# Rows scattered in expert order with token number and gate inside, in a sigmoid-attention, mixture-of-experts and feed-forward chain on one Trainium2 core

## The chip, the core and the metric

One core of a Trainium2 chip runs the whole program. TensorE (PE) multiplies, ScalarE (ACT) and VectorE (DVE) work on the tiles, GpSimd (POOL) does small work and starts the indirect transfers, SyncE (SP) starts the others. Each engine takes its instructions strictly in the order in which they stand; a wait holds up all that stands behind it on that engine. The metric is the device time of one execution in microseconds (us), the median of several runs.

## The reference, cut to what matters

```python
# 4 batches, 12 heads, 448 tokens, head size 64; 1792 tokens of 768 numbers; 8 experts, 1024 wide; FFN 2048 wide
attn = 1 / (1 + exp(-(q @ k.T / 8 - log(448))))
x = rows(attn @ v)                                  # 1792 x 768
logits = normalize(x) @ normalize(expert_emb).T / tau
e = argmax(logits);  gate = softmax(logits)[e]
for each expert e: out[mask] = gate[mask] * (relu(x[mask] @ w1[e]) @ w2[e])
h = out @ w_in;  return (h - tanh(h)) @ w_out
```

All products are done in two-part float32 (a high and a low part, three matmuls for one product).

## The kernel before, in words

**Attention.** 24 pairs of heads, six for each batch, cut into 84 units. A unit is six score matmuls (L230), two sigmoids on ACT (`ah` L237 and `pq` L238), one subtraction on DVE (`al`, L239) and six matmuls with v (L253) three units later. The `al` instructions are a good ruler: one for each unit, counted here from 1 to 84. After each pair its output is turned into token rows (`rows`, L270): PE writes `pr`, DVE copies it into `rec` (112 partitions x 4 rows x 768).

**Routing.** When a batch's sixth pair is done, `route_a` (L394) finds each token's expert; `square` sums squares on ACT; `route_b` (L416) ranks the tokens within their expert with small matmuls (`prank`) and gives `idx`; `gate` (L444) works out the gate. Before, SP writes `rec` to the DRAM table `x_tok` in token order, one further transfer of single words writes the gate behind each row (L466), and POOL scatters the token number, single words again, to `id_reg` in expert order (L441). `ROUTE` and `ROUTE_E` say how many units after `route_a` this is placed; `ROUTE_E` is for the third batch.

**Experts.** Tokens are worked on in groups of 256 of one expert. Two groups are taken from the first three batches, before the fourth is routed (`plan_early`, `early_rows`); the plan for the others (`plan`, L561) is made during the first group. `gather_rows` (L642) fetches, for each half group of 128: the token numbers `gi` from `id_reg`, then the rows `xg` from `x_tok` by these numbers, both indirect from POOL; then ACT multiplies the row by its gate (L658), and SP writes the numbers to `tok_d`, 128 single words. `columns` (L663) transposes the rows on PE, ACT writes the high part `xh` and DVE the low part `xl`. A group (L730) is then 14 products: eight with w1 (18 matmuls each) and six with w2 (24 each), 288 matmuls; for each, ACT casts the weights (`wh`), DVE makes the rest (`wl`), and four such pairs of buffers go round, so ACT is at most four products ahead of PE. In this input nine groups run. SP loads the weights: seven transfers for each group (`w1raw`, `w2raw`).

**What sets the order.** The engines' programs come from a scheduler that simulates the program; only PE's order in the attention is written by hand (units, `plan(u, f)`). While the groups run, ACT and DVE also convert the weights of the last stage (`conv_steps`, L801: `cr` loaded by SP, `ca` on ACT, four steps on DVE, written back). The last stage (`ffn`, L844) reads `toki`, the token numbers in the order of the rows, and scatters the output by it.

Of the kernel before, what the change touches and what calls it, by code (L numbers as in the profile page):

```python
# [10 lines left out]
F32 = mybir.dt.float32  # L11
# [12 lines left out]
ROUTE, ROUTE_E = 8, 8  # L24
# [14 lines left out]
class Prog:  # L39
    def __init__(self, ctx, tc, q, k, v, emb, tau, w1, w2, w_in, w_out, out):  # L40
# [9 lines left out]
        self.R = self.DM + 1  # L50
# [8 lines left out]
    def constants(self):  # L59
# [20 lines left out]
        self.e_off = cp.tile([P, E], F32, name="e_off")  # L80
        nc.gpsimd.iota(self.e_off, [[self.NT, E]], base=0, channel_multiplier=0, allow_small_or_imprecise_dtypes=True)
        self.base = cp.tile([P, E], F32, name="base")
        nc.vector.tensor_copy(self.base, self.e_off)
        self.tok = cp.tile([CP, self.B, NCH], I32, name="tok")
        nc.gpsimd.iota(self.tok, [[self.S, self.B], [1, NCH]], base=0, channel_multiplier=NCH)
# [41 lines left out]
    def attention(self):  # L127
# [93 lines left out]
        def scores(u):  # L221
# [16 lines left out]
            nc.scalar.activation(pv, pv, AF.Sigmoid, **sc)  # L238
            nc.vector.tensor_tensor(lo, pv, f32(hi), ALU.subtract)  # L239

        def av(u):
            hi, lo = tiles.pop(u)
            for x, (i, a, c, o) in enumerate(slots[u]):
# [12 lines left out]
                if e:  # L256
                    b, j = pairs[i]
                    if j == 0:
                        self.bts[b] = dict(
                            rec=xp.tile([CP, NCH, NJ * P], F32, tag="rec", name="rec"),  # L260
                            ss=self.sm.tile([CP, NCH], F32, tag="ss", name="ss"),
                            u=xp.tile([CP, NCH, E], F32, tag="u", name="u"),
                        )
# [6 lines left out]
        def rows(i):  # L270
# [19 lines left out]
            if j >= NJ - 2:  # L290
                c0, c1 = (0, (NJ - 1) * P) if j < NJ - 1 else ((NJ - 1) * P, NJ * P)
                self.x_dma = nc.sync.dma_start(self.x_rows(b)[:, :, c0:c1], rec[:, :, c0:c1])

        def square(bt, c):
            sq = xp.tile([CP, NJ * P], F32, tag="sq", name="sq", bufs=1)
            nc.scalar.activation(sq, bt["rec"][:, c], AF.Square, accum_out=bt["ss"][:, c : c + 1])
# [19 lines left out]
        for i in range(NK):  # L316
            kqs.append(pers.tile([P, KW + S], F32, name=f"kq{i}"))
        kpads()
# [13 lines left out]
        with tc.manual_schedule(engines=pe):  # L332
# [11 lines left out]
            def route(i):  # L344
# [6 lines left out]
                if b == B - 2:  # L351
                    plan(now[0] + ROUTE_E, self.route_b, b, r, pr)
                    plan(now[0] + ROUTE_E, self.gate, b, r)
                    plan(now[0] + ROUTE_E, self.early_rows)
                    plan(ns + 1, self.early_columns, lambda: ps2.tile([P, 2, 512], F32, tag="qk", name="xt"))
                elif b < B - 1:
                    plan(now[0] + ROUTE, self.route_b, b, r, pr)
                    plan(now[0] + ROUTE, self.gate, b, r)
# [57 lines left out]
    def route_b(self, b, st, pst):  # L416
# [6 lines left out]
        for c in range(NCH):  # L423
# [3 lines left out]
            )  # L427
        rk = sm.tile(A3, F32, tag="rk", name="rk")
        nc.vector.tensor_tensor(rk, pr[:CP, :NCH], self.base[:CP].unsqueeze(1).to_broadcast(A3), ALU.add)
        nc.vector.tensor_tensor(rk, rk, oh, ALU.mult)  # L430
        idx = sm.tile([CP, NCH], I32, tag="idx", name="idx")
        with nc.allow_low_precision(reason="whole numbers below 2**24"):
            nc.vector.tensor_reduce(idx, rk, AX.X, ALU.add)
        nc.vector.tensor_tensor(self.base, self.base, pr[:, NCH], ALU.add)
        for c in range(NCH):
            self.scatter(
                self.id_sc,
                out=self.id_reg,
                out_offset=bass.IndirectOffsetOnAxis(ap=idx[:, c : c + 1], axis=0),
                in_=self.tok[:, b, c : c + 1],  # L440
# [3 lines left out]
    def gate(self, b, st):  # L444
# [19 lines left out]
        gt = sm.tile([CP, NCH], F32, tag="gt", name="gt")  # L464
        nc.vector.reciprocal(gt, gs)
        nc.sync.dma_start(self.x_rows(b)[:, :, DM : DM + 1], gt.unsqueeze(2))  # L466

    def x_rows(self, b):
        return self.x_tok[b * self.S : (b + 1) * self.S].rearrange("(p c) r -> p c r", c=NCH)
# [611 lines left out]
```

## Time and profile before

| | before |
|---|---|
| runs shown | 1087.98, 1092.14, 1100.88 us (median 1092.14) |
| profiled execution | 1099.0 us, its span 1097.3 us |
| PE busy in the span | 1028.9 us (94%) |
| mean granted TensorE clock | 0.975 of full speed |
| attention | to about 242 us |
| first expert product starts | 255.36 us |
| last stage starts | 614.55 us |

In the rows below a timeline line is: start, duration, engine, source line, operation, output <- inputs, shape, count, and in brackets the idle time ahead of it with what ended it. All times are us from the start of the span.

### The profile page before, as it was taken

How to read it: one execution, taken by the hardware profiler on the slowest of the kernel's cores; microseconds unless marked ns; L12 is line 12 of the kernel's file. 1: busy time of each engine (PE TensorE's matmuls, PEld its weight loads, DVE VectorE, ACT ScalarE, POOL GpSimd, SP SyncE). 2: the span in 40 equal slices, each digit the busy share in tenths (PEclk: the TensorE clock that was granted, in tenths of full speed). 3: DMA queues.
4: the chain of work that ended last, by engine and by line, in shares of the span. 5: the costliest groups of instructions: out<-in, count | busy, mean ns of one | idle time of the engine just before them, and what ended most of it. 6: DMA issues, size and time to landing. Idle time of an engine off the chain costs nothing. (4 is left out here: it accounts for less than half of the span.)

```text
span 1097.3 us, 16753 instructions
## 1 busy us (share of the span) xinstructions
PE 1028.9 (94%) x6418; PEld 952.1 (87%) x6418; DVE 816.6 (74%) x1093; ACT 557.7 (51%) x693; POOL 185.5 (17%) x191
## 2 busy tenths in 40 slices
PE   6999999867899979979999899999999999999996
PEld 4777777657899979979999799999999999999996
DVE  7888888926578677768886479988898766667773
ACT  6788878636457556556665353344343333322320
POOL 7446454522141111200000000000000300000002
PEclk9999999987989989989999899999999999999999
DMA  5443534069988999999692455444442533322312
GB/s 164 136 133 52 161 51 147 7 58 270 245 224 190 295 260 244 200 200 234 225 317 88 147 201 173 173 173 157 176 134 110 194 137 116 113 93 111 116 58 101
DMA packets 93400, 175.11 MB, mean 160 GB/s; under 512 B 14976, under 2 KB 72064, under 8 KB 93312
## 3 DMA queue, kind: packets, MB, share of 16 engines
q1 hardware_dynamic: 89664, 161.35, 50.4%
q0 software_dynamic: 3648, 12.61, 5.3%
q8 instruction: 53, 0.87, 0.3%
q14 instruction: 35, 0.29, 0.1%
HBM read 156.55 MB, written 36.26 MB: 176 GB/s over the span
## 5 line engine op out<-in xcount | busy, mean ns | idle before, releaser
L953 PE MATMUL o<-wo,gh 128*128 128x384 f32 x896 | 240.5, 335 | 0.7 <-DVE acc L963 0.7
L913 PE MATMUL z<-yh,wi 128*128 128x448 f32 x768 | 222.0, 371 | 4.5 <-ACT yh L888 4.5
L953 PEld LDWEIGHTS o<-wo,gh 128*128 128x128 f32 x896 | 162.9, 188 | 2.3 <-DVE acc L963 1.0
L913 PEld LDWEIGHTS z<-yh,wi 128*128 128x128 f32 x768 | 145.2, 190 | 17.2 <-ACT yh L888 4.7
L953 PE MATMUL o<-wo,gl 128*128 128x384 f32 x448 | 149.8, 334 | 0.0
L725 PE MATMUL pth<-xh,wh 128*128 128x256 f32 x432 | 126.4, 293 | 17.4 <-DVE hl L742 13.4
L913 PE MATMUL z<-yl,wi 128*128 128x448 f32 x384 | 138.3, 368 | 0.0
L725 PE MATMUL pth<-xh,wl 128*128 128x256 f32 x432 | 125.3, 290 | 1.4 <-DVE wl L716 1.4
L725 PE MATMUL pth<-xl,wh 128*128 128x256 f32 x432 | 125.3, 290 | 0.0
L725 PE MATMUL pty<-hh,wh 128*128 128x256 f32 x432 | 122.3, 288 | 2.8 <-ACT hh L741 2.8
L725 PE MATMUL pty<-hl,wh 128*128 128x256 f32 x432 | 122.7, 286 | 1.9 <-DVE hl L742 1.9
L725 PE MATMUL pty<-hh,wl 128*128 128x256 f32 x432 | 122.7, 286 | 0.6 <-DVE wl L716 0.6
L963 DVE TENSOR_TENSOR acc<-o,acc 128x768 f32<-128x768 f32 x98 | 93.6, 955 | 39.5 <-PE o L953 38.3
L239 DVE TENSOR_TENSOR al<-pq,ah 128x896 fp32r<-128x896 f32 x84 | 90.4, 1084 | 34.7 <-ACT pq L238 34.5
L473 POOL DMA_INDIRECT out_dram<-acc,toki x14 | 17.3, 1232 | 577.2 <-DVE acc L963 577.2
L936 ACT CAST gh<-r 128x896 fp32r<-128x896 f32 x32 | 30.1, 941 | 156.6 <-DVE r L934 80.6
L237 ACT ACTIVATE ah<-pq,bias_s 128x896 fp32r<-128x896 f32 x84 | 85.4, 1016 | 41.2 <-PE pq L230 39.8
L725 PEld LDWEIGHTS pth<-xh,wh 128*128 128x128 f32 x432 | 86.1, 199 | 18.8 <-issue 14.2
L716 DVE TENSOR_TENSOR wl<-w1raw,wh 128x768 fp32r<-128x768 f32 x72 | 68.6, 956 | 31.6 <-ACT wh L715 31.1
L716 DVE TENSOR_TENSOR wl<-w2raw,wh 128x1024 fp32r<-128x1024 f32 x54 | 66.1, 1223 | 31.0 <-ACT wh L715 30.6
L725 PEld LDWEIGHTS pth<-xh,wl 128*128 128x128 f32 x432 | 85.8, 199 | 1.9 <-DVE wl L716 1.9
L715 ACT CAST wh<-w2raw 128x1024 fp32r<-128x1024 f32 x54 | 56.5, 1048 | 58.9 <-PE pty L725 24.4
(210 smaller groups left out, 2196.7 us busy)
## 6 DMA issues: line engine op xcount, KB each, us to landing
w1raw<-in_moe_w_dram SPq DMA_DIRECT2D x36, 768.0 KB
w2raw<-in_moe_w_dram SPq DMA_DIRECT2D x27, 1024.0 KB
wi<-dwi SPq DMA_DIRECT2D x32, 768.0 KB
wo<-dwo SPq DMA_DIRECT2D x32, 768.0 KB
cr<-in_moe_w_in_dram SPq DMA_DIRECT2D x16, 768.0 KB
dwi<-cr SPq DMA_DIRECT2D x16, 768.0 KB
cr<-in_moe_w_out_dram SPq DMA_DIRECT2D x16, 768.0 KB
dwo<-cr SPq DMA_DIRECT2D x16, 768.0 KB
```

Of the source, the lines that this page charges most:

```text
L237: nc.scalar.activation(hi, pv, AF.Sigmoid, **sc)
L239: nc.vector.tensor_tensor(lo, pv, f32(hi), ALU.subtract)
L473: i = self.nc.gpsimd.indirect_dma_start(**kw)
L715: nc.scalar.copy(wh, cols)
L716: nc.vector.tensor_tensor(wl, cols, f32(wh), ALU.subtract)
L725: nc.tensor.matmul(pt[:, u], a[:, kk], b[:, kk], start=(n == 0), stop=(n == 3 * K - 1))
L913: nc.tensor.matmul(z[:, g, :GT], wi[:, a, j * P : (j + 1) * P], b[:, j], start=(n == 0), stop=(n == 3 * NJ - 1),)
L936: nc.scalar.copy(gv, r)
L953: nc.tensor.matmul(o[:, w, :NW], a[:, u, i * P : (i + 1) * P], wo[:, b, w * NW : (w + 1) * NW], start=(n == 0), stop=(n == 3 * CH - 1),)
L963: nc.vector.tensor_tensor(acc[i], ov, acc[i], ALU.add)
```

## The change

Rows are no longer written to `x_tok` in token order. `rec` gets 16 more words in each row: word 768 is the token's number, word 769 its gate. POOL scatters these rows of 3136 bytes straight to their place in the batch's expert order (`send_rows`), so SP's writes of `rec`, of the gates and the table `id_reg` go away, and a gather needs one hop, not two. The place of a token in the new table has to be worked out from four batches' tables (`row_of`). The number comes back by a transpose of one column (`row`), and SP writes it as one line of 256 words. `gather_rows` is split: for the first two groups the fetching (`gather_x`) and the multiplication by the gate (`gate_rows`) are placed apart. The weights of the first group no longer wait for its rows. `ROUTE_E` goes from 8 to 3.

```diff
-ROUTE, ROUTE_E = 8, 8
+ROUTE, ROUTE_E = 8, 3
-        self.R = self.DM + 1
+        self.R = self.DM + 16
 # attention: rows()
-            if j >= NJ - 2:
-                self.x_dma = nc.sync.dma_start(self.x_rows(b)[:, :, c0:c1], rec[:, :, c0:c1])
+            if j == 0:
+                nc.gpsimd.tensor_copy(rec[:, :, self.DM : self.DM + 1], self.tok[:, b].unsqueeze(2))
 # route()
-                    plan(now[0] + ROUTE_E, self.gate, b, r)
+                    plan(now[0] + ROUTE_E - 1, self.gate, b, r)
+                    plan(now[0] + ROUTE_E, self.send_rows, b, r)
                     plan(now[0] + ROUTE_E, self.early_rows)
+                    plan(ns, self.early_gates)
+    def send_rows(self, b, st):
+        for c in range(NCH):
+            self.scatter(self.x_sc, out=self.x_tok[: (b + 1) * self.S],
+                out_offset=bass.IndirectOffsetOnAxis(ap=bt["idx"][:, c : c + 1], axis=0), in_=bt["rec"][:, c], ...)
 # gate()
-        nc.sync.dma_start(self.x_rows(b)[:, :, DM : DM + 1], gt.unsqueeze(2))
+        nc.vector.reciprocal(bt["rec"][:, :, DM + 1 : DM + 2], gs.unsqueeze(2))
+    def row_of(self, res, pos, shifts, befores, tmp):
+        V.tensor_copy(s, shifts[0])
+        for x, n in zip(shifts[1:], befores):
+            V.tensor_tensor(d, x, s, ALU.subtract)
+            V.tensor_tensor(y, pos, n, ALU.is_ge)
+            V.tensor_tensor(d, d, y, ALU.mult)
+            V.tensor_tensor(s, s, d, ALU.add)
+        V.tensor_tensor(res, pos, s, ALU.add)
 # plan(): 12 tables are picked from, not 5
+        tabs += [self.shift[:, b] for b in range(B)] + [self.n_before[:, b] for b in range(1, B)]
 # early_rows()
-            self.weight(self.e0, None, c, self.s0["g"])
+            self.weight(self.e0, None, c)
+        for s in (self.s0, self.s1):
+            for h in range(2):
+                self.gather_x(s, h, nt)
+    def early_gates(self):
+        with self.tc.issue_after(self.last_sig.ins):
+            for h in range(2):
+                self.gate_rows(self.s0, h)
 # gather_rows()
-            nc.gpsimd.indirect_dma_start(out=gi[:, h : h + 1], out_offset=None, in_=self.id_reg, ...)
-            nc.sync.dma_start(self.tok_d[o].unsqueeze(1), gi[:, h : h + 1])
 # columns()
+            nc.tensor.transpose(pt[:, h * P : (h + 1) * P], s["x"][:, h, self.DM : self.DM + 1], self.ident)
+        nc.vector.tensor_copy(s["row"], pt)
+    def keep_numbers(self, s):
+        nc.sync.dma_start(self.tok_d[o].unsqueeze(0), s["row"])
 # experts(): for the second group, after the third relu of the first
+        def second():
+            with tc.issue_after(relus[-2].ins):
+                for h in range(2):
+                    self.gate_rows(self.s1, h)
+            self.columns(self.s1, pst)
```

On SP, after the attention's last load of v (`vr`), there stands before:

```order
L183 DMA vr<-in_v_dram 128x512
L466 DMA x_tok<-gt 448x1x1
...
L660 DMA tok_d<-gi 128x1 x2
L660 REGISTER_ALU
L660 DMA tok_d<-gi 128x1
L660 ISA
L660 DMA tok_d<-gi 128x1
L686 ISA
L686 DMA w1raw_144<-in_moe_w_dram 128x6x256
```

and now, where `pe_eo` is the first group's expert from `plan_early`:

```order
L186 DMA vr<-in_v_dram 128x512
L663 TENSOR_LOAD pe_eo_2231
L663 ISA x2
L753 ISA
L753 DMA w1raw_146<-in_moe_w_dram 128x6x256
L753 ISA
L753 DMA w1raw_147<-in_moe_w_dram 128x6x256
L753 ISA
L753 DMA w1raw_148<-in_moe_w_dram 128x6x256
```

The first weights stand directly behind the plan; the four writes of single words ahead of them are gone. On ACT, at the end of the attention, the multiplications by the gate (`xg<-xg`) stand before between the sigmoids of the last two units, and the second group's two ahead of the first group's `xh`:

```order
L658 ACTIVATE xg<-xg 128x768
L237 ACTIVATE ah<-pq,bias_s 128x896
L238 ACTIVATE pq<-pq,bias_s 128x2x448
L658 ACTIVATE xg<-xg 128x768
L237 ACTIVATE ah<-pq,bias_s 128x896
L238 ACTIVATE pq<-pq,bias_s 128x2x448
L658 ACTIVATE xg<-xg 128x768 x2
L676 CAST xh<-xt 128x512 x3
L266 COPY xT<-pav 128x448
L715 CAST wh<-w1raw_144 128x768 x2
```

and now:

```order
L240 ACTIVATE ah<-pq,bias_s 128x896
L241 ACTIVATE pq<-pq,bias_s 128x2x448
L240 ACTIVATE ah<-pq,bias_s 128x896
L241 ACTIVATE pq<-pq,bias_s 128x2x448
L706 ACTIVATE xg<-xg 128x768 x2
L729 CAST xh<-xt 128x512 x3
L269 COPY xT<-pav 128x448
L776 CAST wh<-w1raw_146 128x768 x2
```

No sigmoid stands behind a gathered row, and the second group's multiplications have moved into the first group. On ACT, from the second group's end to the third group's start (`yT` takes a group's result, `xh` is the third group's input), there stands before:

```order
L715 CAST wh<-w1raw_144 128x768
L658 ACTIVATE xg<-xg 128x768 x2
L715 CAST wh<-w1raw_144 128x768
L758 ISA
L758 COPY yT_2686<-pty 128x2x256
L676 CAST xh<-xt 128x512 x2
L715 CAST wh<-w1raw_145 128x768
L813 ACTIVATE ca<-cr 128x768
L715 CAST wh<-w1raw_145 128x768
L758 ISA
L758 COPY yT_2687<-pty 128x2x256
L676 CAST xh<-xt 128x512
```

and now:

```order
L776 CAST wh<-w1raw_147 128x768
L706 ACTIVATE xg<-xg 128x768 x2
L776 CAST wh<-w1raw_147 128x768
L821 ISA
L821 COPY yT_last<-pty 128x2x256
L729 CAST xh<-xt 128x512 x2
L883 ACTIVATE ca<-cr 128x768
L706 ACTIVATE xg<-xg 128x768
L729 CAST xh<-xt 128x512
```

The first two `xh` have moved behind the second group's last `yT`, and a conversion step and one gated row stand ahead of the third.

## Rows read from the trace of the kernel before

**Rows 1.** Page, part 1: busy time, share of the span, instructions.

```profile
PE 1028.9 (94%) x6418; PEld 952.1 (87%) x6418; DVE 816.6 (74%) x1093; ACT 557.7 (51%) x693; POOL 185.5 (17%) x191
```

**Rows 2.** Timeline of PE, end of the attention and first expert group.

```profile
233.04 0.66 PE L253 MATMUL pav<-ah,vh 128*128 128x448 f32 x1 [3.42 <-ACT ah L237]
...
250.63 2.15 PE L278 MATMUL pr<-ien,xT 128*112 128x136 f32 x8 [8.72 <-ACT xT L266]
255.36 0.58 PE L725 MATMUL pth<-xh,wh 128*128 128x256 f32 x1 [2.57 <-ACT wh L715]
```

**Rows 3.** Timeline of ACT, same stretch.

```profile
231.16 0.93 ACT L658 ACTIVATE xg<-xg 128x768 f32<-128x768 f32 x1 [7.58 <-DMA xg<-x_tok,gi]
...
246.62 0.94 ACT L658 ACTIVATE xg<-xg 128x768 f32<-128x768 f32 x1 [9.10 <-DMA xg<-x_tok,gi]
...
254.48 1.57 ACT L715 CAST wh<-w1raw 128x768 fp32r<-128x768 f32 x2 [3.90 <-DMA w1raw<-in_moe_w_dram]
```

**Rows 4.** Timeline of SP's queue, same stretch.

```profile
219.59 24.15 SPq L660 DMA_DIRECT2D tok_d<-gi  x4
243.97 2.20 SPq L686 DMA_DIRECT2D w1raw<-in_moe_w_dram  x3
```

**Rows 5.** Stretches: us, busy us (instructions) of PE, PEld, DVE, ACT, POOL; clock, DMA share, GB/s.

```profile
250.00:260.00 10.00, 6.59 (x27) 5.96 (x28) 5.72 (x11) 5.21 (x9) 0.00 (x0) 0.50 0.88 248
...
500.00:540.00 40.00, 40.00 (x337) 40.00 (x336) 32.12 (x39) 24.96 (x35) 0.00 (x0) 1.00 0.80 218
```

**Rows 6.** Timeline of DVE, third batch's routing: `al` 70 and 71, gate, plan, `al` 78, plan.

```profile
189.09 2.08 DVE L239 TENSOR_TENSOR al<-pq,ah 128x896 fp32r<-128x896 f32 x2
...
203.86 0.17 DVE L465 RECIPROCAL gt<-gs 112x4 f32<-112x4 f32 x1
...
208.99 3.06 DVE L541 TENSOR_SCALAR pe_start<-pe_oh,pe_m 128x8 f32<-128x8 f32 x1
...
213.26 1.08 DVE L239 TENSOR_TENSOR al<-pq,ah 128x896 fp32r<-128x896 f32 x1
214.26 0.14 DVE L519 TENSOR_REDUCE pe_mx<-pe_left 128x1 f32<-128x8 f32 x1
...
215.64 0.22 DVE L555 TENSOR_TENSOR pe_ord<-c_tri,pe_oh 128x64 f32<-128x64 f32 x1
```

**Rows 7.** Timeline of POOL, third batch's scatter and first gather.

```profile
206.11 0.96 POOL L473 DMA_INDIRECT id_reg<-tok,idx  x1 [0.30 <-issue]
...
209.58 2.37 POOL L199 TENSOR_TENSOR w1l<-kq,w1h 128x448 fp32r<-128x448 f32 x2
...
219.83 0.94 POOL L654 DMA_INDIRECT xg<-x_tok,gi  x1 [0.74 <-DMA gi<-id_reg,gidx]
```

**Rows 8.** Transfers into `xg`: us from issue to landing.

```profile
DMA to landing us min/median/max: 7.2/10.4/19.4
```

**Rows 9.** Transfers out to `out_dram`, 128 rows of 3072 bytes: from issue to landing.

```profile
DMA to landing us min/median/max: 3.0/3.4/4.4
```

**Rows 10.** Timeline of PE in the expert groups: a set of transposes, two idle times.

```profile
298.89 0.39 PE L725 MATMUL pth<-xh,wh 128*128 128x256 f32 x1 [1.40 <-ACT wh L715]
...
383.79 1.03 PE L672 MATMUL xt<-ident,xg 128*128 128x128 f32 x8
...
475.78 0.55 PE L725 MATMUL pth<-xh,wh 128*128 128x256 f32 x1 [7.42 <-DVE hl L742]
```

**Rows 11.** Timeline of ACT in the expert groups: two waits for transfers.

```profile
401.08 0.89 ACT L813 ACTIVATE ca<-cr 128x768 f32<-128x768 f32 x1 [5.87 <-DMA cr<-in_moe_w_out_dram]
...
472.39 0.94 ACT L658 ACTIVATE xg<-xg 128x768 f32<-128x768 f32 x1 [8.42 <-DMA xg<-x_tok,gi]
```

**Rows 12.** Timeline of POOL in the expert groups: two gathers' issues.

```profile
305.63 4.87 POOL L654 DMA_INDIRECT xg<-x_tok,gi  x1 [11.24 <-DMA x_tok<-gt]
...
452.97 1.52 POOL L654 DMA_INDIRECT xg<-x_tok,gi  x1 [0.30 <-issue]
```

**Rows 13.** Waits of SP's queue over the span: total us, times, longest.

```profile
SPq L660 <- DMA tok_d<-gi: 60.4, 11, 8.3
```

More of the change, by code (lines that the diff above doesn't have):

```diff
@@ L567, in plan @@
         tn = t("tn", P, 2, E)
[L568 to L569 removed]
+        V.tensor_tensor(tn[:, 1], self.n_before[:, self.B], self.start, ALU.subtract)
         gt = t("gt", P, E, MT)
@@ L605, in plan @@
         gidx = cp.tile([P, NG, 2], I32, name="gidx")
-        V.scalar_tensor_tensor(gidx, b2(ef), float(NT), pos, ALU.mult, ALU.add)
+        self.row_of(
+            gidx, pos, [b2(sums[:, 5 + b]) for b in range(B)], [b2(sums[:, 5 + B + b]) for b in range(B - 1)],
+            t("ro", P, 3, NG, 2),
+        )
         e_i, new, off = (cp.tile([P, NG], I32, name="pl_" + x) for x in ("ei", "new", "off"))
@@ L678, in columns, with weight @@
         s["xt"] = (xh, xl)
-    def weight(self, e, new, c, after=None):
+        pt = pst()[:1, 0, :GR]
+        for h in range(2):
+            nc.tensor.transpose(pt[:, h * P : (h + 1) * P], s["x"][:, h, self.DM : self.DM + 1], self.ident)
+        s["row"] = self.mrow.tile([1, GR], F32, tag="row", name="row")
+        nc.vector.tensor_copy(s["row"], pt)
+    def keep_numbers(self, s):
+        nc, pl = self.nc, s["pl"]
+        o = slice(0, self.GR)
+        if "off" in pl:
+            o = ds(self.reg(nc.sync, pl["off"], s["slot"], self.NT - 1), self.GR)
+        nc.sync.dma_start(self.tok_d[o].unsqueeze(0), s["row"])
+    def weight(self, e, new, c):
         nc = self.nc
@@ L689, in weight @@
         self.last_w = i
-        if after is not None:
-            self.tc.add_manual_dep(
-                i.ins, after.ins.name,
-                mybir.DependencyInfo(mybir.DependencyClass.Sync, mybir.DependencyReason.DATA),
-                reason="rows of the first group before its weights",
-            )
     def experts(self, cx):
@@ L734, in group @@
                 if c >= have:
-                    with tc.issue_after(self.x_dma.ins) if mid is not None else ExitStack():
-                        self.weight(e, new, c)
+                    self.weight(e, new, c)
                 pt = ps.tile([P, 2, GR], F32, tag="h", name="pth")
@@ L780, in last_route @@
             self.route_b(*self.last_route, pst)
+            self.gate(*self.last_route)
+            self.send_rows(*self.last_route)
             pl.update(self.plan())
-            self.gate(*self.last_route)
-        group(self.s0, self.e0, None, slice(0, GR), NWE, lambda: self.columns(self.s1, pst), True, last_route)
+        def second():
+            with tc.issue_after(relus[-2].ins):
+                for h in range(2):
+                    self.gate_rows(self.s1, h)
+            self.columns(self.s1, pst)
+        group(self.s0, self.e0, None, slice(0, GR), NWE, second, True, last_route)
         e, new = (self.reg(nc.sync, self.pl1[x], 0, n) for x, n in (("e", E - 1), ("new", 1)))
@@ L1010, in build @@
                 self.attention()
-            yp = self.pool("yT", 1, side="right")
-            self.yT = [yp.tile([P, 2, self.NT + self.GR], F32, name=f"yT{c}") for c in range(self.NJ // 2)]
+            yp = self.pool("yTb", 1, side="right")
+            self.yT = [yp.tile(ysh, F32, name=f"yT{c}") for c in range(self.NJ // 2 - 1)] + self.yT
             with ExitStack() as cy:
```

142 lines of the change are left out of this document (83 added, 59 removed).

## The prediction, as it went on record

> **What bounds the kernel now.** The page's first part comes first: PE is busy 94% of the span [rows 1], so all that this change can win, short of removing PE work, lies in PE's idle time and in its slow clock. The timeline of PE from the attention's end to the first expert product [rows 2] shows where that is. PE starts a unit late by 3.42 us because ACT had not yet made `ah`; it waits 8.72 us for `xT`, again ACT's; and the first expert product, at 255.36, comes 2.57 us late for ACT's `wh`. So ACT's timeline is read next [rows 3]. ACT itself had nothing to do: at 231.16 it stood 7.58 us, and at 246.62 another 9.10 us, at a multiplication whose row was still in flight, and the sigmoids, the copy of `xT` and the casts stand behind that wait on its queue. Then it waits 3.90 us for the first weights. SP's timeline says why these are late [rows 4]: four writes of token numbers hold the queue from 219.59 for 24.15 us (each waits for its `gi`), and `w1raw` goes out only at 243.97. While PE stood, the clock granted to it fell: 0.50 of full speed in the stretch 250 to 260, against 1.00 in the middle of the groups [rows 5]. There PE does 337 matmuls in 40.00 us, so the 288 of a group take 34.2 us, and nine groups 308. From the first expert product to the last stage (255.36 to 614.55 in the table above) are 359 us: some 51 us are transposes, idle time and half clock. Of them the largest stall is 7.42 us at 475.78 [rows 10], when ACT had stood 8.42 us for a row [rows 11] whose gather POOL issued at 452.97 [rows 12] and which landed 19.4 us later [rows 8].
>
> **The change, step by step.** The sum is made for the profiled execution, 1099.0 us, which lies 6.9 above the median of the runs.
>
> (a) *The way to the first expert product.* ACT's two waits inside the attention go, since no sigmoid stands behind a gathered row any more, and SP's wait ahead of `w1raw` goes with the four writes: the weights are in place some 20 us earlier. What is left is the rows' own way, now: all of the third batch's routing, plan included, gate, four scatters, two gathers, two multiplications, transposes. It begins later than before. Before, the gate was ready at 203.86 and POOL scattered the numbers at 206.11 [rows 6, 7]; now the gate must be inside the row, and in DVE's order its reciprocal stands behind `al` 78, with 85 small operations of routing and plan between `al` 70 and `al` 78 where 33 stood. Before, `al` 78 ran at 213.26; from `al` 70 at 189.09 that is 24.2 us for eight units [rows 6]. The 52 more small operations cost 0.106 us each by the fourteen from 214.26 to 215.64, 5.5 us in all, if nothing hides them; nothing, if DVE had that much slack and no port stall like the 3.06 us of `pe_start` at 208.99, which ran beside POOL's `w1l` [rows 6, 7]. I take four of the 5.5 (DVE is close to full there): gate at 217.3, bounds 213.3 and 222. Four scatters of 0.96 + 0.30 us [rows 7] end at 222; the last lands after 3.4 us, as transfers of 128 rows to `out_dram` do [rows 9], up to 10.4, as gathers do [rows 8]; I take 4, hence 226, since a scatter of rows is most like the former. The two gathers of the first group go out 1.26 apart and need 7.2 to 10.4 [rows 8]; I take 9: the second is there at 236.3. Before, from the last gated row at 246.62 to the first product it is 8.74 us, of which ACT waited 3.90 and PE 2.57 for the weights [rows 2, 3]: without them 4.84 by ACT, 6.17 by PE at half clock. I take 5.5. But there the first group's transposes stood ready; now twelve of them follow the row, at 1.03 / 8 = 0.13 us, 1.5 us [rows 10]. 236.3 + 5.5 + 1.5 gives a first product at 243.3, **-12 us**. With the gate at 222 and landings of 10.4 for scatter and gathers it is 222 + 5 + 10.4 + 1.3 + 10.4 + 7 = 256: +1. With 213.3 and landings of 3.4 and 7.2 it would be 237, where PE's own work is the bound: its last units, two times `pr` and the transposes reach to some 240: -15.
>
> (b) *Numbers by transposes.* Two more in each of nine groups, at full cost on PE: 18 x 0.13 = **+2.3** [rows 10].
>
> (c) *Gathers of the later groups.* One hop instead of two. The row of group five that landed after 19.4 us is asked for without first fetching its number, so about 3.7 us earlier (an issue of 1.52 and the wait for the number, which in a quiet queue is 2 to 4). Of the 7.42 us and some 2 us at half clock behind it, I take half back: **-5**; bounds 0 (the landing is slow again) and -9.4.
>
> (d) *Waits for transfers in the groups.* SP spent 60.4 us of its queue's time in waits for `gi` [rows 13]; with nine line writes of a row that DVE has already made this goes nearly to nothing, and the weights and `cr` behind them leave when their buffers are free. Waits that such transfers end: 5.87 us of ACT at 401.08 for `cr` [rows 11], behind the 1.40 of PE at 298.89 [rows 10] and several like it. I take **-6**; bounds 0, since the buffers and not SP may set the time of issue (DMA engines are busy 0.80 of the middle of the groups [rows 5]), and -12.
>
> (e) *The third group's start.* Its `xh` now stand behind the second group's last `yT`, with a conversion step and a gated row ahead of the third; the plan's `gidx` come later. Nothing covers that: PE has no product of another group there. Two casts, a gate of 0.94 and `ca` of 0.89 [rows 11] are 3 to 5 us on the path: **+5**; bounds 0 and +12 (a gather that lands in 10.4 instead of 7.2, and a half clock after the stall).
>
> (f) *Longer plan on DVE.* Some 25 operations for `row_of`, about 0.2 us each with what lies between (0.22 at 215.64 [rows 6]), behind DVE's work at 32.12 of 40.00 us [rows 5]: hidden but for **+1**; 5 without cover.
>
> Sum: -12 + 2.3 - 5 - 6 + 5 + 1 = -14.7, so 1084 for an execution like the profiled one. Part of the stalls in (c) and (d) is late landings, which differ between executions; I take 4 us of them as absent in the median one. That leaves -10.7 from 1092.1: **1081 us**.
>
> A page speaks against the four scatters from POOL. The Trainium skill, page "SBUF — State Buffer", section "SBUF: two separate sides", says that the descriptors of a transfer issued by GpSimd are written by GpSimd itself, through a port pair that VectorE can hold for a whole instruction, so that such a transfer may sit waiting for VectorE. The issue of 0.96 us at 206.11, in a stretch in which DVE is nearly full, does not show it; that of 4.87 us at 305.63 [rows 7, 12] might. By the page the issues would be longer where DVE is busy; the rival C below has the time.
>
> **The rivals.** *B, the rows come no earlier.* The scatter waits for a gate that stood 13 us earlier before, and each row makes two trips of 3 KB where a number made one. With the gate at 222 and a landing of 10.4 for the gathers alone, the first product starts at 222 + 5 + 4 + 1.3 + 10.4 + 7 = 250: -6 instead of -12, and with half of (c) and (d) the sum is about -6 + 2.3 - 5 + 5 + 1 = -3: 1089. This is also the case in which the change doesn't do what it says. For it: DVE's eight units took 24.2 us already. Against: the first weights' 3.90 us go in any case.
>
> *C, slower: POOL's issues stretch.* Six indirect issues stand one behind the other ahead of the first group. At 4.87 us each [rows 12] in place of 1.26 they take 22 us more: first product at 265, +10, sum +7 with all else as forecast, and +18 with nothing of (c) and (d): 1099 to 1110. It decides from about 12 / 6 = 2 us more for each issue, where the gain of (a) is gone. For it: one issue of 4.87 and one of 1.52. Against: 0.94 and 0.96 at 204 to 220, in the same stretch [rows 7].
>
> *D, ACT is held at the head of each later group.* The gates of groups three to six stand in ACT's program some products ahead of the group's end, and all of ACT's casts stand behind them. A landing of 19.4 [rows 8] instead of 10.4 costs 3 to 7 us a group; over four groups +12 to +28 less the 7.42 already paid: 1085 to 1101. It decides when landings near 19 us are the rule rather than the longest.
>
> **How the numbers follow.** The forecast (first product 240 to 247, later stalls reduced) has 0.5, B 0.25, C 0.1, D 0.15. The likeliest gives 1081, its own range is 1070 to 1087: from (a) at -15 with (c) and (d) near their better ends, to (a) at -9 with a little less of (c) and (d). The range reaches up through B and the lower half of D: 1066 to 1096, leaving out C, the upper half of D, and a little below. About 1% is what a measurement of this kernel can tell from no change: 1081.2 and 1103.1 are the borders. Since the forecast lies at the first of them, faster takes some six tenths of its 0.5 and a part of B and D where the group's waits shrink more: 0.45. Slower is most of C and a third of D: 0.14; the rest 0.41.
>
> **What would show it.** (a) PE's idle time behind `ah` and `xT` is gone and the first expert product starts near 243; POOL's scatters begin near 217 and take about 1 us each; `w1raw` is issued near 220. If the first product starts after 250, B or C holds: B if the gate is late or the landings are long, C if the issues are. (c) No idle of 7 us ahead of a later group's `xh`. (d) SP waits little at the number writes; ACT's waits for `cr` under 2 us. (e) The third group's first product comes up to 5 us late. The forecast is wrong as a whole if DVE between `al` 70 and `al` 78 takes over 35 us, if a scatter of rows lands after 15, or if the groups, from first product to the last stage, take more than the 359 us of before.

## The result, and the profile after

The changed kernel takes 1057.4 us (median of 1055.1 to 1058.5) against 1096.3 for the kernel before beside it (1088.0 to 1100.9): a ratio of 0.965, 95% interval 0.958 to 0.972. The forecast was 1081 with a range of 1066 to 1096. The direction was right and the size was not: 39 us were gained where 11 were forecast. The kernel before was timed again beside each of the six sets of experiments below, at 1105.1 to 1117.7; the changed kernel in its second timing took 1057.2 us. Why the kernel before varies so much between sets, and the changed one does not, no run tells. Each experiment is compared with the kernel before of its own set, by the ratio, and with the 1057 of the changed kernel, which mostly comes from another set.

Busy time of the engines in the span, after (the answer to [rows 1]):

```profile
PE 1019.5 (96%) x6437; PEld 943.1 (89%) x6437; DVE 828.6 (78%) x1170; ACT 558.7 (53%) x693; POOL 175.3 (17%) x178
```

The timeline of PE, the first expert product and the longest idle time in the groups (answers to [rows 2, 10]):

```profile
238.76 1.18 PE L281 MATMUL pr<-ien,xT 128*112 128x136 f32 x8 [0.68 <-ACT xT L269]
239.69 0.37 PE L786 MATMUL pth<-xh,wh 128*128 128x256 f32 x1
...
314.79 0.50 PE L786 MATMUL pth<-xh,wh 128*128 128x256 f32 x2 [1.17 <-ACT xh L729]
```

The first product comes at 239.69, 15.7 us earlier, and the last stage starts at 575.30. In the nine groups PE waits 1.17 us at most, once, at the third group's start; ahead of the last stage it waits 5.13 us (4.54 before). The way to the first product, on POOL (last scatter, first group's two gathers), ACT (their gates) and SP (first weights), answers to [rows 3, 4, 7]:

```profile
223.02 0.94 POOL L491 DMA_INDIRECT x_tok<-rec,idx  x1 [0.30 <-issue]
227.60 0.99 POOL L698 DMA_INDIRECT xg<-x_tok,gidx  x1 [2.19 <-DMA x_tok<-rec,idx]
228.90 0.96 POOL L698 DMA_INDIRECT xg<-x_tok,gidx  x1 [0.30 <-issue]
```

```profile
231.75 0.94 ACT L706 ACTIVATE xg<-xg 128x768 f32<-128x768 f32 x1
233.15 0.94 ACT L706 ACTIVATE xg<-xg 128x768 f32<-128x768 f32 x1 [0.46 <-issue]
```

```profile
198.14 1.59 SPq L753 DMA_DIRECT2D w1raw<-in_moe_w_dram  x3
```

ACT waits for no row and no weight. SP's queue, however, stands as long at the number writes as before (60.4 us, [rows 13]), now for the row of numbers:

```profile
SPq L745 <- DVE row L737: 67.2, 8, 32.0
```

The time went like this, in the profiled executions; the third column is an experiment, told of below, in which only the distance of the numbers in DRAM differs from the kernel before:

| | before | after | before, words 64 bytes apart |
|---|---|---|---|
| first expert product | 255.4 | 239.7 | 238.1 |
| nine groups, to the last stage | 359.2 | 335.6 | 334.8 |
| last stage | 482.7 | 481.5 | 483.0 |
| span | 1097.3 | 1056.8 | 1055.8 |

### The profile page after: what moved, and what is told of

It is laid out like the page before. It is cut to its first block, busy times and chain, and to the rows that moved or that the text cites. A ratio compares the mean times of both kernels' runs of the same rounds, so it can differ in the third digit from the quotient of the medians.

```text
span 1056.8 us, 16798 instructions
## 1 busy us (share of the span) xinstructions
PE 1019.5 (96%) x6437; PEld 943.1 (89%) x6437; DVE 828.6 (78%) x1170; ACT 558.7 (53%) x693; POOL 175.3 (17%) x178
## 4 chain that ended last, share of the span: by engine, by line
issue 56%; PE 31%; DVE 7%; POOL 2%; DMA 2%; ACT 1%; POOLq 0%; SPq 0%; DVEq 0%; ACTq 0%
PE pth L786 9%; PE pty L786 9%; PE pav L256 7%; PE pq L233 5%; POOL out_dram L491 2%; DVE al L242 1%; PE pr L281 1%; DMA xg<-x_tok,gidx 1%; DVE vh L210 1%; PE xt L725 1%; DMA cr<-in_moe_w_in_dram 1%; ACT wh L776 0%; DVE xT L271 0%; ACT sq L298 0%; POOL vl L211 0%
## 5 line engine op out<-in xcount | busy, mean ns | idle before, releaser
L786 PE MATMUL pth<-xh,wh 128*128 128x256 f32 x432 | 122.6, 285 | 2.7 <-ACT xh L729 1.2
L786 PE MATMUL pth<-xh,wl 128*128 128x256 f32 x432 | 122.3, 283 | 0.3 <-DVE wl L777 0.3
L786 PE MATMUL pth<-xl,wh 128*128 128x256 f32 x432 | 122.2, 283 | 0.0
L995 ACT ACTIVATE t<-z 128x896 f32<-128x896 f32 x32 | 29.4, 920 | 112.3 <-PE z L988 75.8
L786 PEld LDWEIGHTS pth<-xh,wh 128*128 128x128 f32 x432 | 82.7, 192 | 3.3 <-ACT xh L729 1.4
```

Of the source, the lines that this page charges most:

```text
L786: nc.tensor.matmul(pt[:, u], a[:, kk], b[:, kk], start=(n == 0), stop=(n == 3 * K - 1))
```

## Experiments

**First set: which part gave the groups 23.6 us?** Four kernels, the kernel before at 1117.7 us. The theories A to M in the expectations have letters of their own; they are not the rivals B to D of the prediction. Of each edit the lines that matter are shown.

The numbers written again as single words from the gathered rows:

```diff
+        self.nc.sync.dma_start(self.tok_d[o].unsqueeze(1), s["x"][:, h, self.DM : self.DM + 1])
-            self.keep_numbers(s)
```

> The changed kernel, but the token numbers go to tok_d as before: 128 single words from each half group, written by SP straight from the gathered rows, so that SP waits for each gather (the transposes of the numbers stay, their row isn't written). Three theories of where the groups' 23.6 us came from (335.6 us from the first expert product to the last stage, 359.2 before). A, SP's waits for gathered rows hold the weights and cr behind them: +10 to +18 us, the groups at 346 to 354 us, with PE idle again behind ACT's waits for cr. B, single words are expensive for the DMA engines that carry them: +8 to +15, but as much in the run with words that wait for nothing. C, the second hop of a gather made rows late and held ACT: within 2 us of the changed kernel, 1055 to 1060.

Measured: 1104.5 us, ratio 0.988 (0.985 to 0.991). Of the 60 us by which this set's kernel before is slower than the changed kernel 47 are back, 2.6 times the most that a theory had allowed. First product 239.4, groups 385.4. SP hardly waits for rows (1.4 us); it waits 44.0 us for the landing of its own words.

Words that wait for nothing, added to the changed kernel:

```diff
+                self.nc.sync.dma_start(self.junk[k : k + P].unsqueeze(1), self.ident[:, :1])
```

> The changed kernel with work added: for each half group SP also writes 128 single words, from a constant tile to a place of its own, so that nothing is waited for. Every other engine's program is as in the changed kernel. A (SP's waits): within 2 us, 1055 to 1060. B (single words load the DMA engines): +8 to +15, the groups at 344 to 351 us, and the DMA share in the groups several hundredths up. C (second hop): within 2 us.

Measured: 1070.7 us, but not as meant: since the source is ready early, SP issued all 18 transfers at 23.6 to 64.7, among the attention's first loads. The groups stayed at 335.8, and the attention lost the time: first product 252.3. So it says nothing of words in the groups, but 2304 words that nobody reads or waits for cost 12.6 us there.

The second hop back:

```diff
+        self.nc.gpsimd.indirect_dma_start(out=gi, out_offset=None, in_=self.id_reg,
+            in_offset=bass.IndirectOffsetOnAxis(ap=s["pl"]["gidx"][:, s["slot"], h : h + 1], axis=0))
-            in_offset=bass.IndirectOffsetOnAxis(ap=s["pl"]["gidx"][:, s["slot"], h : h + 1], axis=0),
+            in_offset=bass.IndirectOffsetOnAxis(ap=gi, axis=0),
```

> The changed kernel with the second hop back: each half group's indices are first fetched, indirectly, as 128 single words from a table that holds 0, 1, 2 and so on, and the rows are then fetched by what came back. Output unchanged. First expert product 4 to 8 us later for the hop (all theories). In the groups: A (SP's waits): nothing, total 1061 to 1066. B (single words): about +4, half of the words of before come back. C (second hop makes rows late and holds ACT): +9 to +15, PE idle 2 to 8 us ahead of xh of some groups, total 1070 to 1080.

Measured: 1065.5 us, some 8 over the changed kernel. First product 240.2, groups 340.8, with one idle time of 5.21 us ahead of a group's transposes. Theory C falls: the hop costs the groups 5 us, and is not where 23.6 us went.

The kernel before without its writes to `tok_d`:

```diff
-            nc.sync.dma_start(self.tok_d[o].unsqueeze(1), gi[:, h : h + 1])
```

> The kernel before without its 18 writes of single words to tok_d: the table is filled once at the start with 0, 1, 2 and so on (so the last stage's output rows go to wrong places; the work is the same). SP no longer waits for gi. A (SP's waits): the first product 2 to 5 us earlier, groups 12 to 18 us shorter, total 1073 to 1083. B (single words): groups 4 to 8 us shorter, total 1083 to 1090. C (second hop): groups the same but for the buffer of gi, which no longer waits for the write, total 1085 to 1095.

Measured: 1068.6 us, ratio 0.957 (0.952 to 0.961). The kernel without the writes sends its output to wrong rows, with the same work otherwise. Eighteen transfers of half a kilobyte each are worth 49 us to the kernel before. First product 245.6, groups 337.1. What remained to be found was what in them costs so much.

**Second set: the wait or the words?** By now I had read [rows 13] again. Its 60.4 us are not waits for `gi`: the row names `tok_d<-gi`, the landing of the write before, at places of the same table. The wait for `gi` has a row of its own, here from the same view:

```profile
SPq L660 <- DMA gi<-id_reg,gidx: 3.7, 2, 2.9
```

In SP's timeline a second half's number write follows the first's after 13 us; other transfers go out between, and for the last 2.9 us the queue waits for the first write to land:

```profile
316.02 0.37 SPq L660 DMA_DIRECT2D tok_d<-gi  x1
...
329.04 0.35 SPq L660 DMA_DIRECT2D tok_d<-gi  x1
```

> The changed kernel itself, beside the three that follow, since the kernel before was 1117.7 us beside the first four experiments and 1096.3 before that. All theories: 1055 to 1062 us. If the kernel before depends on the chip through its waits for single words and the changed one does not, this stays at 1057 while the kernel before moves.

Measured: 1057.2 us, ratio 0.956 (0.953 to 0.960), the kernel before at 1106.0.

One write for each group in the kernel before:

```diff
-            nc.sync.dma_start(self.tok_d[o].unsqueeze(1), gi[:, h : h + 1])
+        nc.sync.dma_start(self.tok_d[o].rearrange("(h p) -> p h", p=P), gi)
```

> The kernel before with one write of numbers for each group instead of two: the same 256 single words, the same gathers ahead of it, but no second write that has to wait until the first one has landed. D (SP is held by a write that waits for the landing of the write before it, at places of the same table): SP's waits for tok_d fall from 60 us to under 15, and the time comes near that of the kernel without these writes, 1065 to 1085. B (the words themselves load the DMA engines): at most 8 us below the kernel before. A as I first put it (SP waits for gi): at most 5 us below the kernel before, since gi is waited for as ever.

Measured: 1079.7 us, ratio 0.978 (0.974 to 0.982); SP's waits for `tok_d` fell to 11.5 us. About half of the gain, with as many words: between D and B. But it does not separate the two: the two words of one partition now stand side by side in the transfer and 128 words apart in DRAM, so their order is another too.

Words from the gathered rows, each to a place of its own:

```diff
+        self.nc.sync.dma_start(self.junk[k : k + P].unsqueeze(1), s["x"][:, h, self.DM : self.DM + 1])
```

> The changed kernel with work added: SP writes the number of each gathered row as single words, as in the run with words in tok_d, so that it waits for every gather, but each to a place of its own, so that no write waits for another. D (wait of write on write): 1057 to 1066, SP waits for xg and little else. A (waits for gathered rows): near the run with words in tok_d, +30 to +47, 1090 to 1105. B (words): +5 to +15.

Measured: 1081.8 us, ratio 0.978 (0.974 to 0.982). No write waits for a write, SP's waits for rows are 6.8 us in all, and still it is 25 us slower.

Words behind the line of numbers:

```diff
+            nc.sync.dma_start(self.junk[k : k + P].unsqueeze(1), f32(s["xt"][0][:, h, :1]))
```

> The changed kernel with work added: 256 single words for each group, written behind the line of numbers from a tile that is ready then, each to a place of its own, so that SP waits for nothing more (the earlier run of this kind issued its words during the first attention units and not in the groups). D: 1057 to 1062. A: 1057 to 1062. B (words load the DMA engines): +5 to +15, DMA share in the groups up.

Measured: 1060.0 us, +3. As many words cost 3 or 25 us, by where they stand. Left were the wait for rows, and the loads among which the words go out.

**Third set: that wait alone, words among loads alone, and two parts of the way to the first product.** The kernel before at 1105.1 us.

```diff
+        self.nc.sync.dma_start(self.junk[k : k + 16].unsqueeze(0), s["x"][:1, h, self.DM : self.DM + 16])
```

> The changed kernel with a small transfer added at the places of the run whose words were written from the gathered rows to places of their own: for each half group SP writes 16 words of one row, 64 bytes, to a place of its own, so SP waits for each gather as in that run, but no 128 words follow. E (a wait of SP for gathered rows is what cost that run its 25 us): 1075 to 1085. F (the words cost it, by what they do to the loads between which they stand): 1056 to 1062.

Measured: 1056.4 us. SP waits 45.9 us for gathered rows, and it costs nothing:

```profile
SPq L704 <- DMA xg<-x_tok,gidx: 45.9, 8, 25.4
```

E falls, and with it theory A, that waits for rows hold up the loads behind them.

```diff
+                if c < 2:
+                    nc.sync.dma_start(self.junk[k : k + P].unsqueeze(1), f32(hh[:, 2 * c, :1]))
```

> The changed kernel with 256 single words added for each group, as in the earlier run with words behind the line of numbers (+3 us), but written from the first two activations of the group (hh), so that they stand among the loads of weights and cr, and not behind them; SP waits for no gather. E: 1056 to 1063. F (words among loads): +12 to +25, 1069 to 1082, issues on SP that last several us, ACT waiting for cr.

Measured: 1071.7 us, +14.6. F holds. The same stretch of 200 us in the middle of the groups, in the changed kernel, with waits alone, and with words among the loads (us, then busy us and instructions of PE, PEld, DVE, ACT, POOL; granted clock, DMA share, GB/s):

```profile
300.00:500.00 200.00, 198.02 (x1656) 197.02 (x1655) 166.20 (x205) 134.66 (x181) 23.67 (x10) 1.00 0.73 250
```

```profile
300.00:500.00 200.00, 198.02 (x1656) 197.01 (x1656) 167.60 (x206) 134.08 (x180) 25.71 (x10) 1.00 0.73 248
```

```profile
300.00:500.00 200.00, 190.75 (x1563) 188.49 (x1562) 153.45 (x193) 126.17 (x172) 10.54 (x10) 0.98 0.90 252
```

PE loses 7 us of work, at the same GB/s, while the DMA share, the share of time in which the transfer engines have a packet in hand, rises from 0.73 to 0.90.

The first weights wait for the rows again:

```diff
+                    self.tc.add_manual_dep(self.last_w.ins, g.ins.name, ...)
```

> The changed kernel with one part undone: the first group's three weight transfers wait for its gathered rows again, as before. Programs of PE, ACT, DVE and POOL as in the changed kernel. By the sum of the prediction: the weights land some 11 us after the rows instead of long before, first expert product 5 to 9 us later, total 1062 to 1067. Rival: the weights' wait was only due to the four writes of numbers ahead of them; then under 2 us, 1056 to 1059.

Measured: 1060.2 us, +3: less than the sum, more than the rival. The first product is not later (237.5; in profiles of kernels that are the same up to there it comes at 236.6 to 239.7), but ACT waits 1.25 and 2.05 us for the first weights.

```diff
-ROUTE, ROUTE_E = 8, 3
+ROUTE, ROUTE_E = 8, 8
```

> The changed kernel with ROUTE_E back at 8: the third batch's ranking and scatter are planned five units later. If the rows' own way sets the first expert product, it comes about five units (12 us) later, less the 2 to 3 us by which the rows are early now: total 1064 to 1069. If PE's work in the attention sets it, under 3 us: 1056 to 1060.

Measured: 1061.8 us, +4.7; first product 243.8. ACT waits 3.03 and 1.30 us for rows, and PE behind it. But the edit does not do what was meant: the ranking moved back and the gate moved ahead, so the scatters begin at 216.7, earlier than the 219.2 of the changed kernel, and only the plan is late; the first gather goes out at 228.8 in place of 227.6, and the two gates run 0.9 and 1.7 us later. What a scatter five units later would cost is not shown.

**Fourth to sixth set: what is it in the words?** The run with words among the loads is repeated with other packets at the same places. In those with 8 and 64 bytes and with distances, all engines run the same instructions in the same order; in the one with 512 bytes some stand elsewhere.

```diff
-                    nc.sync.dma_start(self.junk[k : k + P].unsqueeze(1), f32(hh[:, 2 * c, :1]))
+                    nc.sync.dma_start(self.junk[k : k + P], f32(hh[:, 2 * c, :16]))    # rows of 16 words; 128 in the next
```

> The run with words written from hh (256 packets added for each group, 1071.7 us against 1057.2 of the changed kernel), with 64 bytes in each packet in place of 4, to a table of its own. G (the number of packets or their smallness counts): +10 to +20 as with words, 1067 to 1077. H (a single word is what is slow): under 4 us, 1056 to 1061.

> The same with 512 bytes in each packet (128 KB for each of 18 transfers, 2.4 MB in all, about 1.4% more than the kernel moves). G by number: +10 to +20 again, 1067 to 1077. G by size (packets under some size are slow): under 5 us, 1057 to 1062, though eight times the bytes of the run with 64. H: under 4 us.

Measured: 1056.9 and 1059.8 us. The number of packets costs nothing; with 512 bytes it is +2.6, for 64 KB a transfer, 1.2 MB in all (the expectation has both twice too large).

```diff
+                    nc.sync.dma_start(self.junk[k : k + P, :1], f32(hh[:, 2 * c, :1]))     # rows of 16 words: 64 bytes apart
+                    nc.sync.dma_start(self.junk[k : k + P], f32(hh[:, 2 * c, :2]))         # the other run: 8 bytes each
```

> The run with 256 single words from hh added for each group (1071.7 us), but each word is written 64 bytes from the next, into a table of its own; programs of all five engines as there. J (the word's size is what costs): +10 to +16, 1067 to 1073. K (neighbouring words in one stretch of memory, written by several transfer engines at once, hold each other up): under 4 us, 1056 to 1061.

> The same places with 8 bytes in each packet, next to each other. J with a limit at one word: under 4 us, 1056 to 1061. J with the cost falling with size: +5 to +12. K: nearly as with words, +8 to +14, 1065 to 1071.

Measured: 1057.4 and 1057.9 us. A single word is not slow: 64 bytes apart it costs nothing, and the two kernels with 1071.7 and 1057.4 differ in nothing but the distance of the words in DRAM. J falls. K holds for the distance, not for the pairs of 8 bytes, which touch each other and cost no time.

```diff
+                    nc.sync.dma_start(self.junk[k : k + P, :1], f32(hh[:, 2 * c, :1]))     # rows of 2 words: 8 bytes apart
```

> The run with 256 single words added for each group (1071.7 us when 4 bytes apart, 1057.4 when 64 apart), now 8 bytes apart; programs of all five engines as in both. If neighbours within a short stretch of memory hold each other up: +8 to +14, 1065 to 1071. If only words that touch each other do: under 3 us, 1056 to 1060.

Measured: 1056.0 us. Eight bytes apart is enough for the time. The share of the transfer engines in the same 200 us shows more than the time does: 0.73 without added packets, 0.90 with touching words, and these, of words 8 bytes apart, and of words 64 bytes apart:

```profile
300.00:500.00 200.00, 198.03 (x1656) 197.01 (x1655) 165.73 (x205) 134.70 (x182) 23.89 (x10) 1.00 0.78 254
```

```profile
300.00:500.00 200.00, 198.03 (x1656) 197.01 (x1655) 165.43 (x205) 134.69 (x181) 23.89 (x10) 1.00 0.74 250
```

Last, the kernel before with its numbers 64 bytes apart, every instruction on every engine in its old place, the second hop, the order and all (a third line, not shown, reads them back at that distance):

```diff
-        self.tok_d = dp.tile([self.NT + self.GR], I32, name="tok_d")
+        self.tok_d = dp.tile([self.NT + self.GR, 16], I32, name="tok_d")
-            nc.sync.dma_start(self.tok_d[o].unsqueeze(1), gi[:, h : h + 1])
+            nc.sync.dma_start(self.tok_d[o, :1], gi[:, h : h + 1])
```

> The kernel before with 64 bytes in tok_d for each token number in place of 4: the same transfers of the same words in the same order on every engine, 64 bytes apart (the last stage reads them back with that distance). L (neighbouring words cost the kernel before its time): -25 to -48 against the kernel before, near the kernel without these writes, 1058 to 1080; SP's waits for tok_d fall from 60 us to under 30. M (it is the number of transfers or the wait as such): under 5 us below the kernel before, 1100 to 1106.

Measured: 1060.0 us (1057.6 to 1062.7), ratio 0.957 (0.953 to 0.962), the kernel before at 1109.1. L holds, and touching words cost the kernel before 49 us. The same 200 us of the kernel before and of this one:

```profile
300.00:500.00 200.00, 181.42 (x1451) 180.14 (x1452) 147.23 (x177) 119.43 (x161) 36.85 (x24) 0.95 0.97 235
```

```profile
300.00:500.00 200.00, 200.00 (x1676) 199.93 (x1676) 162.52 (x195) 134.36 (x179) 25.11 (x20) 1.00 0.78 257
```

PE goes from 181 to 200 busy us of 200. Its SP wait for landings of number writes (60.4 before, [rows 13]), its gathers' time from issue to landing (7.2/10.4/19.4 before, [rows 8]), and the first group's first gather and gate (219.83 and 231.16 before, [rows 3, 7]):

```profile
SPq L660 <- DMA tok_d<-gi: 3.6, 2, 2.6
```

```profile
DMA to landing us min/median/max: 3.9/6.3/9.2
```

```profile
220.48 0.95 POOL L654 DMA_INDIRECT xg<-x_tok,gi  x1 [0.75 <-DMA gi<-id_reg,gidx]
```

```profile
224.39 0.94 ACT L658 ACTIVATE xg<-xg 128x768 f32<-128x768 f32 x1 [0.72 <-DMA xg<-x_tok,gi]
```

The gather goes out at the same time as before, and its row is used 7 us earlier. So other transfers land late when touching words are written beside them. Over the span ACT's waits for rows fall from 28.0 to 3.6 us, those for `cr` from 39.2 to 22.3, those for weights from 12.8 to 6.5, and SP's for its own words from 60.4 to 3.6. How much of the 49 us comes through late loads, and how much through SP's queue, which stands behind its own late words, these runs do not separate.

So of the 39 to 49 us that the changed kernel gains, all but some 3 or 4 come from no longer writing numbers as touching words: 1060.0 against the 1057.2 of another set, or against 1056.0 in the same set for the changed kernel with added words 8 bytes apart. The rest of the change, with its gate inside the row, its one hop, `ROUTE_E` and the freed weights, is worth about that much when the words are out of the way. No run beats the changed kernel by more than a measurement can tell.

## Why the prediction was wrong, step by step

**The step that failed is (d)**, with a misreading behind it. I put "SP spent 60.4 us of its queue's time in waits for `gi`", and earlier "each waits for its `gi`". The row said `tok_d<-gi`, the landing of a write; for `gi` itself SP waited 3.7 us. From the misreading it followed that SP's queue was the thing to free, at -6 us with a bound of -12. SP's queue was not freed: it stands 67.2 us at the number writes in the changed kernel, and that costs nothing. What went was the touching words, and with them the late landings beside them. From (b) to (f) the forecast for the groups was -2.7; with every term at its best bound it was some -19. The measured -23.6 lies outside even that. With (b), (c) and (e) as they are read below, some -22 of it are left for (d). The sign to stop at was a queue that stands 60.4 us in all behind the landing of writes of 512 bytes.

**(a), first product 243.3.** 239.7 was measured, -15.7 where -12 was forecast, outside the step's bounds of -15 and +1 by 0.7. Its parts: the gate at 218.7 where 217.3 was forecast. That it came so near is luck: `al` 70 came 4.1 us later than in the profile of before (193.21 against 189.09; 189.9 in the profiles of two experiments with nearly the same program up to there), while the eight units from `al` 70 to `al` 78 took 24.5 us against 24.2, so the 52 small operations cost hardly any of the 4 us put down for them. Last scatter to gather 4.6 us where 4 to 5 were; second gather to its gate 4.25 us at most where 9 were; from there to the first product 6.5 where 7 were (the 8.74 us behind those 7 were counted from 246.62 as the last gated row; one more was gated at 247.77). The term that was mis-sized is the gathers' landing. I took 9 from [rows 8], and these 7.2 to 19.4 us were the price under touching words; in the changed kernel it is 4.5/7.0/10.8. A price was carried over from a state that the change itself ends. The new order on ACT and SP is not needed for the gain: in the kernel before with its words spread, nothing else moved, the first product comes at 238.1.

The first group's own rows came hardly earlier. Before, its gates ran at 231.16 [rows 3] and here:

```profile
234.82 0.94 ACT L658 ACTIVATE xg<-xg 128x768 f32<-128x768 f32 x1 [0.97 <-DMA xg<-x_tok,gi]
```

After, they ran at 231.75 and 233.15. The wait at 246.62, which stood ahead of the first product, was for the second group's rows; it left the path in the changed kernel by the new order, and in the kernel with spread words because those rows had landed by 232.6.

**(b), +2.3.** A quiet group takes 36.06 us after, and 35.85 in the kernel before with spread words: 9 x 0.21 = 1.9. The size was right.

**(c), -5.** The whole 7.42 went, and mostly not for the hop, as I argued: with the hop in place and the words spread the longest landing is 9.2 us, and with the hop put back into the changed kernel a group waits 5.21 us, once.

**(e), +5.** The third group starts with the idle time of 1.17 us shown above. From the middle of the second group, its first product with w2 at 295.31, to that of the third at 334.93 are 39.6 us, and 36.0 from there to the next: +3.6, of which eight more transposes are about 1. The direction was right, and the size nearly.

**(f), +1.** The largest wait on that side is 0.90 us of PE on `ls`, which belongs to the routing; no run shows the longer plan's cost apart.

**The 4 us taken off** for late landings "as absent in the median one" are shown by no run: beside the changed kernel the median of before was 1096.3, 2.7 below the profiled execution, and in all later sets it was above it, at 1105 to 1118.

**The rivals of the prediction.** B, that the rows come no earlier, holds for the first group's first row and nearly for its second (1.7 us earlier), but its price, a first product at 250, does not follow: the gathers landed sooner than it allowed, and what had held the product was the second group's rows and the weights. C: the scatters and first gathers took 0.94 to 1.02 us each; four gathers of 4.36 us in later groups held up nobody. The Trainium skill's page "SBUF — State Buffer", section "SBUF: two separate sides", on which C leant, speaks of some of VectorE's instructions and not of VectorE being busy. At those scatters and gathers DVE was busy 8.9 of 14 us, less full than C's argument had it (19.4 of 20 at 200 to 220 before), so the stretch hardly puts that rule to the test. D: no landing over 10.8. None of the rivals named the transfer engines themselves, though the share of 0.80 in [rows 5] was quoted as a reason against a gain. Part of it was the symptom: in the changed kernel the same stretch, 500 to 540 before and 460 to 500 after by the groups' course, has 0.50, with fewer bytes moved too (176 against 218 GB/s):

```profile
460.00:500.00 40.00, 40.00 (x337) 39.94 (x336) 32.83 (x41) 26.21 (x36) 0.00 (x0) 1.00 0.50 176
```

## What to carry to other kernels

A column of single words written to neighbouring places of DRAM, one from each partition, can slow the transfers beside it; look for 4-byte elements in a transfer's shape before looking at waits, and try the cheapest repair first: spread the words in memory (8 bytes apart was enough here) or turn the column into one line. Before a landing time or a DMA share is carried into a forecast, ask what in the present kernel makes it so long, and whether the change takes just that away: here 7.2/10.4/19.4 us became 3.9/6.3/9.2 by a distance in memory. And read the releaser's name in a row of waits to its end: `tok_d<-gi` and `gi<-id_reg` are different transfers.

## What the runs showed of the hardware that was not expected

Touching words lengthen the packets of other transfers, not their own. The same 82190 packets of SP's queue, 2304 of them added words that touch, or added packets of 64 bytes (packets, MB, share of 16 engines over spans of 1068.1 and 1055.4 us):

```profile
q1 hardware_dynamic: 82190, 155.79, 48.0%
```

```profile
q1 hardware_dynamic: 82190, 155.92, 43.4%
```

That is 8203 against 7329 engine-us, or 0.38 us for each touching word, if all of the difference is put down to them. In the kernel before, the same sum over its 2304 numbers (50.4% of 16 x 1097.3 against 47.0% of 16 x 1055.8) gives 0.39. But a word's own packet is as short in both. The single packets of SP's queue in the traces show where the time is:

| | mean of a 4-byte packet | packets over 1 us, and their sum | sum of all others |
|---|---|---|---|
| changed kernel | 9 ns | 59, 80 us | 7202 us |
| added words 64 bytes apart | 9 ns | 85, 98 us | 7281 us |
| added words 8 bytes apart | 9 ns | 164, 236 us | 7281 us |
| added words that touch | 9 ns | 386, 941 us | 7264 us |
| kernel before, 64 bytes apart | 9 ns | 197, 346 us | 7594 us |
| kernel before | 9 ns | 579, 1206 us | 7635 us |

With added words that touch, the 386 long packets are all of 1024 and 6144 bytes, packets of other transfers, and the longest takes 9.0 us; the average packet of the changed kernel (1957 bytes) takes 0.09. So some 300 packets of the loads and stores beside the words stand for 1 to 9 us, and the rest go as ever. Whether an engine is held by its words, or the memory by all of them, these records do not tell. What that costs PE depends on the place: 3 us for 256 words a group behind the line of numbers, 14.6 among the loads of weights and `cr`, 25 a little earlier, behind the gathers.

The Trainium skill, "DMA: Bandwidth & Descriptors", section "Specifications", says that below 512 bytes the engine reads, modifies and writes. By that rule alone packets of 64 bytes and words far apart should cost as touching words do; the runs put them at -0.2 and +0.2 us against 14.6, so here the measurement decides, and the size of a packet alone is not what costs.

Open is why touching matters. Words 8 bytes apart, and pairs of words that touch (8 bytes each), cost no time, but they have some long packets too (236 and 281 us in packets over 1 us, against 98 with words 64 bytes apart), so the effect seems to fall with distance and not to end where words cease to touch; a shared stretch of 64 bytes is not ruled out. Whether neighbouring writers hold each other up in memory, or a run of touching words is cut differently among the engines, no run here tells. Also open is what share of the 23 us between words with and without a write that waits for another (1104.5 and 1081.8, in different sets) is the wait itself: it wasn't tried with spread words in the changed kernel.
